# Attention against a small state and a feed-forward block on one core: the order of the first loads and of batch 0's preparation is changed

## The chip, the core and the metric

The kernel runs on one core of a Trainium2 chip. A core has TensorE (PE in the profile: matmuls and transposes), VectorE (DVE), ScalarE (ACT), GpSimd (POOL) and SyncE (SP), each with its own instruction queue that it works off in order, and 16 DMA engines that carry out the transfers which SP, GpSimd and ScalarE issue. The metric is the time of one execution on the device in microseconds: the median of several runs.

## What is computed

For each of B = 8 batches and H = 8 heads, x (512 tokens x 64) attends to a state of 32 rows x 64, and the state attends to x. Both results, 544 rows per batch, go through a feed-forward block with a SiLU.

```python
scores = scale * x @ state.T            # per batch and head
a      = softmax(scores)                # over the 32 state rows
xread  = a @ state                      # 512 rows
a2     = softmax(scale * state @ x.T)   # over the 512 tokens
sread  = a2 @ x                         # 32 rows
y      = concat([xread, sread])         # 544 rows x 512
out    = silu(y @ w_in) @ w_out         # w_in 512 x 2048, w_out 2048 x 512
```

x, state and the weights arrive in fp32, the matmuls run in bf16, and the output is fp32, 4352 x 512.

## The kernel before

The 512 tokens of a batch and the hidden width of 2048 are tiled into 4 token tiles (tt) and 16 hidden tiles (ft) of 128. Instead of computing xread and multiplying it by w_in, the kernel multiplies the state of a batch by w_in first (**W1**, lines 356 to 387: state rows x 2048) and then the attention weights by W1 (**G1**, lines 396 to 430, ending in a SiLU on ScalarE). **G2** (line 432) multiplies by w_out and accumulates over the 16 hidden tiles in PSUM; `store` evicts and writes a token tile. A batch has 32 G1 matmuls and 64 G2 matmuls of 512 columns.

Ahead of that stand, per batch: x in fp32 loaded into the one buffer `x_f` (line 102; `load_x`, line 104, issued by GpSimd), its cast to bf16 (`cast_x`, line 118), its transpose (by TensorE for batches 0 and 1, `pe_transpose_x`, line 203; by a DMA transpose on SP's queue from batch 2 on, `transpose_x`, line 131), the scores (line 252), the exponentials on ScalarE (line 266), the normalization `norm` (line 276: sums and reciprocals on VectorE, the multiplication on GpSimd unless told otherwise) and the transpose of the normalized weights into aT (lines 295 and 300). The 32 state rows of the second result (`sread`, line 309) are gathered over all batches and pass the feed-forward block at the very end.

The schedule is manual: each engine gets its instructions in the order in which the program emits them, and a tile framework adds the waits between engines. So the place of a call in the text sets its place in the queue of its own engine, and no more than that. x_f is one buffer: x of batch b+1 can be loaded only when the casts of batch b have read it. One engine's `pers` buffers hold the states: `st0_f` and `st0_n` for batch 0 alone (loaded by SP ahead of x, line 163), `st_b` for all batches (loaded by GpSimd at line 179, behind the first weights), and `stT`, the transposed states in a block layout, filled by `evict_state` (line 234).

The weights are loaded in pieces by GpSimd, with a conversion to bf16, in this order: w_in 0 to 255, w_out tiles 0 and 1, w_in 256 to 511, w_out 2 and 3, w_in 512 to 1023, w_out 4 to 7, all states, then (behind the first normalization) w_in 1024 to 1535, w_out 8 to 11, w_in 1536 to 2047, w_out 12 to 15, then x of batch 1 (lines 173 to 181 and 492 to 496).

Batch 0 runs in the loop of line 513 with three of its token tiles: at hidden tiles ft 0, 2, 6 and 10 a piece of W1 of batch 0 is made, at 5 all states are transposed by TensorE, at 6 and 8 they are evicted by VectorE, at 9, 11 and 12 three pieces of W1 of batch 1 are made, at 12 VectorE casts x of batch 1 and x of batch 2 is loaded, and at 14 x of batch 1 is transposed. Then follow the scores of batch 1, the fourth token tile (line 553) with the casts and the DMA transpose of x of batch 2 and the load of x of batch 3, and the loop of line 569 over batches 1 to 7, in which the next batch n = b + 1 is prepared at fixed places (tt, ft): scores at (0, 16 - lead), normalization, casts and the next load at (1, 0), the padded copy of x for sread at (1, 4), sread and W1 at (2, 4) and (3, 4), the DMA transpose of x at (3, 8).

`bank` (line 72) deals the PSUM banks a0 to a3 out in turn to scores, W1 pieces and transposes; within the loop of batch 0 it has three, as a0 holds the third token tile. `keep_busy` issues matmuls on zeros.

Of the kernel before, what the change touches and what calls it, by code (L numbers as in the profile page):

```python
# [41 lines left out]
def kernel(  # L42
# [36 lines left out]
    st0_f = pers.tile([NS, H, D], FP32)  # L79
    st0_n = pers.tile([NS, H, D], BF16)  # L80
# [23 lines left out]
    def load_x(b):  # L104
        nc.gpsimd.dma_start(x_f[:], x[b].rearrange("h (p c) d -> p h c d", p=128, c=4))  # L105
# [54 lines left out]
    busy = pers.tile([128, 512], BF16)  # L160
    nc.vector.memset(warm[:], 0.0)
    nc.scalar.activation(warm[:], warm[:], func=EXP, bias=0.0)
    nc.sync.dma_start(st0_f[:], state[0].rearrange("h n d -> n h d"))
    for hg in range(2):
# [4 lines left out]
    nc.vector.memset(busy[:], 0.0)  # L169
    nc.vector.memset(stT[:, 0], 0.0)  # L170
    nc.vector.memset(stT[:, 1:8], 0.0)
    make_identity(nc, ident)
    load_w_in(0, 256)
    load_w_out(0, 2)
    load_w_in(256, 256)
    load_w_out(2, 2)
    load_w_in(512)
    load_w_out(4, 4)
    nc.gpsimd.dma_start(
        st_b[:], state.rearrange("b h (n2 m v) d -> (b h n2) m (v d)", n2=2, m=8)  # L180
    )


    keep_busy(4, psH, "h1")
    copy(nc.vector, st0_n[:], st0_f[:])
    ps0 = bank([128, 4, NS], BF16, "ps_st0")
    for kt in range(4):
        nc.tensor.transpose(
            ps0[:, kt, :], st0_n[:, ds(2 * kt, 2), :], ident[0:NS, 0:NS]
        )  # L190
    for g in range(2):
        for u in range(2):
            copy(
                nc.vector,
                stT[ds(64 * u, 64), 0, ds(2 * g, 2), u ^ g, :],
                ps0[ds(64 * u, 64), ds(2 * g, 2), :],
            )
    keep_busy(5, psH, "h1")
# [18 lines left out]

    cast_x(0, nc.vector, 0, 2, 0, 4)
    cast_x(0, nc.scalar, 2, 2, 0, 4)
    pe_transpose_x(0, 0, 2, lambda sh, dt, nm: psO.tile(sh, dt, tag="o", name=nm))  # L220
    cast_x(0, nc.vector, 0, 2, 4, 4)
    cast_x(0, nc.vector, 2, 2, 4, 4)
# [11 lines left out]
    def evict_state(u, eng):  # L234
        to = stT.rearrange("p b k s (n m v) -> p b k s n m v", n=2, m=8)
        for g in range(2):
            for v in range(2):
                copy(
                    eng,
                    to[ds(64 * u, 64), ds(1, B - 1), ds(2 * g, 2), u ^ g, :, :, v],  # L240
                    st_ps[0][
                        ds(64 * v, 64), :, ds(1, B - 1), ds(2 * g, 2), u, :
                    ].rearrange("p m b k n -> p b k n m"),
                )
# [7 lines left out]
    def scores(b, hg):  # L252
        ps = bank([128, 4, 4, NS], FP32, "ps_sc")
        sc_ps[hg] = ps
        for c in range(4):
            for j in range(2):
                nc.tensor.matmul(  # L257
                    ps[:, c, ds(2 * j, 2), :],
# [7 lines left out]
    def exps(b, hg, n=4):  # L266
        e = epool.tile([128, 4, 4, NS], BF16, tag="exp", name="exp_nat")
        exp_nat[b, hg] = e
        for c in range(0, 4, n):
            nc.scalar.activation(  # L270
                e[:, ds(c, n)], sc_ps[hg][:, ds(c, n)], func=EXP, bias=0.0, scale=SCALE
            )
# [27 lines left out]
    def pe_transpose_a(b, hg, eng):  # L300
# [3 lines left out]
        copy(eng, aT[b][:, hg, :, :], ps[:])  # L304
# [104 lines left out]
    def emit_G1(k):  # L409
# [20 lines left out]
        nc.scalar.activation(g[:, 0:n], ps[:, 0:n], func=SILU, bias=0.0)  # L430
# [51 lines left out]
    pe_transpose_x(0, 1, 2, new_h, (nc.vector, nc.vector), (0,))  # L482
    scores(0, 0)
    exps(0, 0)
    pe_transpose_x(0, 1, 2, new_h, (nc.vector, nc.vector), (1,))
    scores(0, 1)
    exps(0, 1, 2)
    norm(0, 0)
    norm(0, 1, ((nc.vector, 0, 3), (nc.gpsimd, 3, 1)), 2)
# [6 lines left out]
    load_x(1)  # L496
    for i in (1, 2, 0):
        ones_beside_x(i, nc.gpsimd)
    keep_busy(4, psO, "o")
    pe_transpose_a(0, 0, nc.vector)  # L500
    keep_busy(2, psO, "o")
    pe_transpose_a(0, 1, nc.vector)
# [6 lines left out]
    turn[0] = 2  # L509
# [3 lines left out]
    for ft in range(NFT):  # L513
# [4 lines left out]
        if ft == 5:  # L518
            transpose_state()
        if ft == 6:  # L520
            evict_state(0, nc.vector)
        if ft == 8:
            evict_state(1, nc.vector)
        if ft == 12:
            cast_x(1, nc.vector)
            load_x(2)
# [126 lines left out]
```

## Time and profile before

| | us |
|---|---|
| median of 7 runs | 221.33 |
| lowest and highest | 219.98, 224.02 |
| the profiled execution, its own time | 221.62 |
| its span, first to last instruction | 219.8 |

The profile is of one execution. A part of a stage that each engine is busy, and the two chains that lead to the end, are shown with the prediction. Three more facts of the page are of use:

| what | number |
|---|---|
| G2 matmuls (line 438) | 494 recorded, 379 ns each, pipelined |
| HBM read over the span | 17.37 MB |
| DMA transposes of x, issue to landing, least, median and most of six | 3.8, 7.6, 9.8 us |

In such a profile the busy time of an engine says how much it worked, not whether anyone waited for it. In the chain of waits each step is followed back to what released it; in the list of instructions the bracket at the end of a line gives the idle time ahead of the instruction and what ended it. SPq and POOLq are the queues of SP and GpSimd that issue transfers.

### The profile page before, as it was taken

Reading aid. Unit: us, or ns where it says so; the run is one execution under the profiler, and the core shown is the slowest. Engines: PE = TensorE matmul, PEld = TensorE weight load, DVE = VectorE, ACT = ScalarE, POOL = GpSimd, SP = SyncE. Lnnn points to the kernel's source line nnn. Section 1 sums busy time; section 2 is a strip of 40 time slices with the busy share of each in tenths; the row PEclk is TensorE's granted clock in tenths of the full one; section 3 lists DMA queues with packets and bytes.
Section 4 is the critical chain, followed back from the end, with each engine's and each line's share of the span. In section 5 each row is a group of like instructions: output and inputs, shape, how many; then the busy total and the mean of one; then the engine's idle time right before and its main releaser. Section 6 shows DMA issues by size and latency. Waiting matters only on the chain.

```text
span 219.8 us, 3943 instructions
## 1 busy us (share of the span) xinstructions
PE 207.4 (94%) x1577; PEld 97.8 (44%) x1603; DVE 74.4 (34%) x167; ACT 142.6 (65%) x242; POOL 48.3 (22%) x70
## 2 busy tenths in 40 slices
PE   7699899996999999999999999999999999999993
PEld 2334335443444443444444444444444444466662
DVE  5830848301571064306321452136211734200011
ACT  3664579899366975698478938794779666734410
POOL 8490002700820045003700180008000400000000
PEclk9999999999999999999999999999999999999999
DMA  6999955596379025911594158703610331011112
GB/s 185 207 207 206 208 195 162 176 133 205 95 205 223 22 69 125 288 55 48 119 246 121 48 95 237 157 23 113 159 51 0 95 104 48 0 48 51 48 48 95
DMA packets 33489, 27.05 MB, mean 123 GB/s; under 512 B 21440, under 2 KB 27328, under 8 KB 33472
## 3 DMA queue, kind: packets, MB, share of 16 engines
q1 hardware_dynamic: 26656, 15.01, 25.4%
q0 software_dynamic: 6816, 11.80, 24.9%
q8 instruction: 12, 0.20, 0.4%
q14 instruction: 5, 0.04, 0.1%
HBM read 17.37 MB, written 8.91 MB: 120 GB/s over the span
## 4 chain that ended last, share of the span: by engine, by line
PE 78%; DMA 11%; DVE 3%; POOL 2%; issue 2%; ACT 1%; SPq 0%; POOLq 0%
PE o L438 46%; PE h L400 19%; DMA w_in_sb<-in_moe_w_in_dram 5%; DMA xT<-x_nat 4%; PE ps_w L367 4%; PE h L419 3%; DMA x_f<-in_x_dram 2%; PE ps_sc L257 2%; PE o_half L460 2%; DVE stT L149 1%; POOL an L286 1%; PE ps_sr L319 1%; POOL x_nat L149 1%; PE ps_xt L211 1%; DVE W L149 1%
## 5 line engine op out<-in xcount | busy, mean ns | idle before, releaser
L438 PE MATMUL o<-w_out_sb,g 128*128 128x512 bf16 x494 | 132.9, 379 | 2.2 <-issue 1.1
L430 ACT ACTIVATE g<-h 128x512 bf16<-128x512 f32 (+1 forms) x144 | 82.1, 573 | 34.9 <-PE h L400 20.6
L438 PEld LDWEIGHTS <-g 128*128 128x128 bf16 x528 | 49.9, 98 | 59.6 <-issue 6.5
L400 PE MATMUL h<-aT,W 128*128 128x512 bf16 x250 | 74.2, 379 | 0.3
L149 DVE COPY o_sb<-o 128x512 f32<-128x512 f32 x17 | 11.7, 691 | 92.1 <-PE o L438 92.1
L286 POOL TENSOR_TENSOR an<-exp_nat,rc 128x512 bf16<-128x512 bf16 (+2 forms) x16 | 18.5, 1175 | 105.1 <-DVE rc L284 102.2
L400 PEld LDWEIGHTS <-W 128*128 128x128 bf16 x256 | 24.7, 97 | 31.2 <-issue 1.9
L149 DVE CAST W<-ps_w 128x512 bf16<-128x512 f32 (+1 forms) x31 | 20.5, 678 | 35.9 <-PE ps_w L367 35.9
L147 ACT ACTIVATE W<-ps_w 128x512 bf16<-128x512 f32 (+1 forms) x35 | 18.7, 577 | 8.8 <-PE ps_w L367 8.7
L147 ACT ACTIVATE o_sb<-o 128x512 f32<-128x512 f32 x15 | 8.9, 596 | 20.4 <-issue 9.1
L149 POOL CAST x_nat<-x_f 128x512 bf16<-128x512 f32 x24 | 13.7, 606 | 0.9 <-DMA x_f<-in_x_dram 0.9
L367 PE MATMUL ps_w<-w_in_sb,stT 64*32 64x512 bf16 (+1 forms) x264 | 11.4, 376 | 0.8 <-DVE stT L149 0.4
L283 DVE TENSOR_REDUCE rs<-exp_nat 128x16 f32<-128x512 bf16 (+1 forms) x17 | 10.5, 625 | 0.9 <-ACT exp_nat L270 0.2
L105 POOL DMA_DIRECT2D x_f<-in_x_dram x7 | 6.5, 926 | 18.9 <-DVE x_rows L149 17.4
L270 ACT ACTIVATE exp_nat<-ps_sc 128x512 bf16<-128x512 f32 (+1 forms) x17 | 8.8, 569 | 2.0 <-PE ps_sc L257 2.0
L419 PE MATMUL h<-xmT,w_in_sb 128*128 128x256 bf16 x64 | 9.6, 273 | 0.1
L419 PEld LDWEIGHTS <-w_in_sb 128*128 128x128 bf16 x64 | 6.3, 98 | 3.9
L585 ACT ACT_TABLE_LOAD x6 | 7.7, 1283 | 0.1
L270 ACT ACT_TABLE_LOAD x6 | 7.7, 1283 | 0.1
L257 PE MATMUL ps_sc<-stT,xT 128*128 128x64 bf16 x128 | 5.4, 193 | 1.9 <-DMA xT<-x_nat 1.7
L257 PEld LDWEIGHTS <-xT 128*128 128x128 bf16 x128 | 4.8, 98 | 4.2 <-DMA xT<-x_nat 2.2
L155 PE MATMUL ps_busy<-busy 128*128 128x512 bf16 x14 | 5.3, 497 | 1.3 <-DVE busy L169 1.2
(55 smaller groups left out, 86.5 us busy)
## 6 DMA issues: line engine op xcount, KB each, us to landing
out_dram<-o_sb SPq DMA_DIRECT2D x33, 256.0 KB, 2.5
x_f<-in_x_dram POOLq DMA_DIRECT2D x7, 1024.0 KB, 6.9
w_in_sb<-in_moe_w_in_dram POOLq DMA_DIRECT2D x3, 512.0 KB, 10.1
w_out_sb<-in_moe_w_out_dram POOLq DMA_DIRECT2D x3, 512.0 KB, 11.9
x_f<-in_x_dram SPq DMA_DIRECT2D x2, 512.0 KB, 5.0
w_in_sb<-in_moe_w_in_dram POOLq DMA_DIRECT2D x2, 256.0 KB, 6.7
w_out_sb<-in_moe_w_out_dram POOLq DMA_DIRECT2D x2, 256.0 KB, 7.2
st_b<-in_state_dram POOLq DMA_DIRECT2D x1, 256.0 KB, 12.0
```

The lines of the kernel that those rows point to most:

```text
L147: nc.scalar.activation(dst, src, func=COPY, bias=0.0)
L149: eng.tensor_copy(dst, src)
L257: nc.tensor.matmul(ps[:, c, ds(2 * j, 2), :], xT[b][:, c, 2 * hg + j, :], stT[:, b, 2 * hg + j, :, :], start=True, stop=True, skip_group_c ...
L270: nc.scalar.activation(e[:, ds(c, n)], sc_ps[hg][:, ds(c, n)], func=EXP, bias=0.0, scale=SCALE)
L283: nc.vector.tensor_reduce(rs[:, ds(c, nr)], e[:, ds(c, nr)], axis=AX, op=ADD)
L286: eng.tensor_tensor(a[:, ds(c, n)], e[:, ds(c, n)], rc[:, ds(c, n)].to_broadcast([128, n, 4, NS]), op=MULT,)
L367: nc.tensor.matmul(pss[f, hg][ds(32 * s, 32), 0:n], stT[ds(r, 64), b, h // 2, s % 2, :], w_in_sb[ds(r, 64), h // 2, ds(f, n)], start=True, ...
L400: nc.tensor.matmul(h_ps[k][:], W1[b][:, hg, ds(128 * ft, 128)], aT[b][:, hg, :, :], start=(hg == 0), stop=(hg == 1), skip_group_check=True,)
L419: nc.tensor.matmul(ps[:, 0:256], w_in_sb[:, kt, ds(128 * ft, 128)], xmT[:, :, kt].rearrange("p t n b -> p t (n b)"), start=(kt == 0), stop ...
L430: nc.scalar.activation(g[:, 0:n], ps[:, 0:n], func=SILU, bias=0.0)
L438: nc.tensor.matmul(outs[tt][:], gt[b * NFT + ft][:, ds(128 * tt, 128)], w_out_sb[:, ft, :], start=(ft == 0), stop=(ft == NFT - 1), skip_gr ...
L585: nc.scalar.activation(warm[:], warm[:], func=SILU, bias=0.0)
```

## The change

In the head:

- SP's first issue is x of batch 0. State 0 is issued by ScalarE ahead of its table load, in another layout (128 partitions x 2 rows), cast by VectorE, transposed by one matmul and placed into stT by four copies on ScalarE. Seven and two busy matmuls stand where four and five stood.
- The ones beside x of batch 0 are set by GpSimd ahead of the weight loads instead of later.
- State 1 is loaded alone, converted, behind w_out 2 and 3. The load of all states stands behind x of batch 1, which comes as two loads.
- ScalarE casts a quarter more of x of batch 0; both first evictions of its transpose are VectorE's, and of the last two one is ScalarE's. The second half of the scores goes to two PSUM banks, its multiplication wholly to VectorE, and the eviction of its transposed weights is split between VectorE and ScalarE. The SiLU of the first hidden tile is issued in two halves.

In batch 0: state 1 is transposed and placed at ft 4; the pieces of W1 of batch 1 are made at 5, 9 and 11; x of batch 1 is cast in two halves at 13; both its transposes are evicted by VectorE.

In the loop: all states are transposed and evicted in batch 1 at (0, 1); `load_x(3)` stands behind the scores and exponentials of batch 2; the second half of each normalization is multiplied by VectorE; the padded copy stands at (0, 4).

```diff
@@ -76,8 +76,9 @@
 
     ident = pers.tile([128, 128], BF16)
     st_b = pers.tile([128, 8, 2 * D], BF16)
-    st0_f = pers.tile([NS, H, D], FP32)
-    st0_n = pers.tile([NS, H, D], BF16)
+    st0_f = pers.tile([128, 2, D], FP32)
+    st1_n = pers.tile([128, 2, D], BF16)
+    st0_n = pers.tile([128, 2, D], BF16)
 
     stT = pers.tile([128, B, 4, 2, NS], BF16)
     w_in_sb = pers.tile([128, 4, DF], BF16)
@@ -101,8 +102,10 @@
 
     x_f = pers.tile([128, H, 4, D], FP32)
 
-    def load_x(b):
-        nc.gpsimd.dma_start(x_f[:], x[b].rearrange("h (p c) d -> p h c d", p=128, c=4))
+    def load_x(b, h0=0, nh=H):
+        nc.gpsimd.dma_start(
+            x_f[:, ds(h0, nh)], x[b, ds(h0, nh)].rearrange("h (p c) d -> p h c d", p=128, c=4)
+        )
 
     def ones_beside_x(i, eng):
         eng.memset(
@@ -158,44 +161,60 @@
 
     warm = pers.tile([128, 1], FP32)
     busy = pers.tile([128, 512], BF16)
+    nc.vector.memset(busy[:], 0.0)
     nc.vector.memset(warm[:], 0.0)
+    nc.scalar.dma_start(
+        st0_f.rearrange("p v d -> p (v d)"),
+        state[0].rearrange("h (m v) d -> (h m) (v d)", v=2),
+    )
     nc.scalar.activation(warm[:], warm[:], func=EXP, bias=0.0)
-    nc.sync.dma_start(st0_f[:], state[0].rearrange("h n d -> n h d"))
     for hg in range(2):
         nc.sync.dma_start(
             x_f[:, ds(4 * hg, 4), :, :],
             x[0, ds(4 * hg, 4)].rearrange("h (p c) d -> p h c d", p=128, c=4),
         )
-    nc.vector.memset(busy[:], 0.0)
     nc.vector.memset(stT[:, 0], 0.0)
     nc.vector.memset(stT[:, 1:8], 0.0)
     make_identity(nc, ident)
+    ones_beside_x(0, nc.gpsimd)
     load_w_in(0, 256)
     load_w_out(0, 2)
     load_w_in(256, 256)
     load_w_out(2, 2)
+    nc.gpsimd.dma_start(
+        st1_n.rearrange("p v d -> p (v d)"),
+        state[1].rearrange("h (m v) d -> (h m) (v d)", v=2),
+    )
     load_w_in(512)
     load_w_out(4, 4)
-    nc.gpsimd.dma_start(
-        st_b[:], state.rearrange("b h (n2 m v) d -> (b h n2) m (v d)", n2=2, m=8)
-    )
-
-
-    keep_busy(4, psH, "h1")
+
+    def load_states():
+        nc.gpsimd.dma_start(
+            st_b[:], state.rearrange("b h (n2 m v) d -> (b h n2) m (v d)", n2=2, m=8)
+        )
+
+    def transpose_one_state(st):
+        ps = bank([128, 2, 2, 2, 16], BF16, "ps_st1")
+        nc.tensor.transpose(
+            ps.rearrange("p g k u m -> p (g k u m)"), st.rearrange("p v d -> p (v d)"), ident[:]
+        )
+        return ps
+
+    def place_one_state(b, ps, eng):
+        flat = stT.rearrange("p b k s n -> p (b k s n)")
+        to = (
+            flat[0:64, ds(256 * b, 320)].rearrange("p (g w) -> p g w", g=2)[:, :, 0:128],
+            flat[64:128, ds(256 * b + 32, 192)].rearrange("p (g w) -> p g w", g=2),
+        )
+        for u in range(2):
+            by_n = to[u].rearrange("p g (k m v) -> p g k m v", m=16, v=2)
+            for v in range(2):
+                copy(eng, by_n[:, :, 0:3:2, :, v], ps[ds(64 * v, 64), :, :, u, :])
+
+    keep_busy(7, psH, "h1")
     copy(nc.vector, st0_n[:], st0_f[:])
-    ps0 = bank([128, 4, NS], BF16, "ps_st0")
-    for kt in range(4):
-        nc.tensor.transpose(
-            ps0[:, kt, :], st0_n[:, ds(2 * kt, 2), :], ident[0:NS, 0:NS]
-        )
-    for g in range(2):
-        for u in range(2):
-            copy(
-                nc.vector,
-                stT[ds(64 * u, 64), 0, ds(2 * g, 2), u ^ g, :],
-                ps0[ds(64 * u, 64), ds(2 * g, 2), :],
-            )
-    keep_busy(5, psH, "h1")
+    ps0 = transpose_one_state(st0_n)
+    keep_busy(2, psH, "h1")
 
 
 
@@ -215,11 +234,13 @@
                     )
             copy(engs[u], xT[b][:, ds(m * u, m), ds(2 * hg, 2), :], ps[:])
 
+    place_one_state(0, ps0, nc.scalar)
     cast_x(0, nc.vector, 0, 2, 0, 4)
     cast_x(0, nc.scalar, 2, 2, 0, 4)
-    pe_transpose_x(0, 0, 2, lambda sh, dt, nm: psO.tile(sh, dt, tag="o", name=nm))
+    new_o = lambda sh, dt, nm: psO.tile(sh, dt, tag="o", name=nm)
+    cast_x(0, nc.scalar, 2, 2, 4, 4)
+    pe_transpose_x(0, 0, 2, new_o, (nc.vector, nc.vector))
     cast_x(0, nc.vector, 0, 2, 4, 4)
-    cast_x(0, nc.vector, 2, 2, 4, 4)
 
     st_ps = []
 
@@ -237,9 +258,9 @@
             for v in range(2):
                 copy(
                     eng,
-                    to[ds(64 * u, 64), ds(1, B - 1), ds(2 * g, 2), u ^ g, :, :, v],
+                    to[ds(64 * u, 64), ds(2, B - 2), ds(2 * g, 2), u ^ g, :, :, v],
                     st_ps[0][
-                        ds(64 * v, 64), :, ds(1, B - 1), ds(2 * g, 2), u, :
+                        ds(64 * v, 64), :, ds(2, B - 2), ds(2 * g, 2), u, :
                     ].rearrange("p m b k n -> p b k n m"),
                 )
 
@@ -249,13 +270,14 @@
     W1 = {}
     sc_ps = {}
 
-    def scores(b, hg):
-        ps = bank([128, 4, 4, NS], FP32, "ps_sc")
-        sc_ps[hg] = ps
+    def scores(b, hg, m=4):
+        sc_ps[hg] = []
         for c in range(4):
+            if c % m == 0:
+                sc_ps[hg].append(bank([128, m, 4, NS], FP32, "ps_sc"))
             for j in range(2):
                 nc.tensor.matmul(
-                    ps[:, c, ds(2 * j, 2), :],
+                    sc_ps[hg][-1][:, c % m, ds(2 * j, 2), :],
                     xT[b][:, c, 2 * hg + j, :],
                     stT[:, b, 2 * hg + j, :, :],
                     start=True,
@@ -263,13 +285,12 @@
                     skip_group_check=True,
                 )
 
-    def exps(b, hg, n=4):
+    def exps(b, hg):
         e = epool.tile([128, 4, 4, NS], BF16, tag="exp", name="exp_nat")
         exp_nat[b, hg] = e
-        for c in range(0, 4, n):
-            nc.scalar.activation(
-                e[:, ds(c, n)], sc_ps[hg][:, ds(c, n)], func=EXP, bias=0.0, scale=SCALE
-            )
+        n = 4 // len(sc_ps[hg])
+        for i, ps in enumerate(sc_ps[hg]):
+            nc.scalar.activation(e[:, ds(n * i, n)], ps[:], func=EXP, bias=0.0, scale=SCALE)
 
     an = {}
 
@@ -297,11 +318,15 @@
             aT[b][:, hg, :, :], an[b, hg][:].rearrange("p c s n -> p (c s n)")
         )
 
-    def pe_transpose_a(b, hg, eng):
+    def pe_transpose_a(b, hg, eng, other=None):
         ps = bank([128, 4, 128], BF16, "ps_at")
         for c in range(4):
             nc.tensor.transpose(ps[:, c, :], an[b, hg][:, c, :, :], ident[:])
-        copy(eng, aT[b][:, hg, :, :], ps[:])
+        if other is None:
+            copy(eng, aT[b][:, hg, :, :], ps[:])
+        else:
+            copy(eng, aT[b][:, hg, 0:2, :], ps[:, 0:2])
+            copy(other, aT[b][:, hg, 2:4, :], ps[:, 2:4])
 
 
     xm_ps = {}
@@ -427,7 +452,9 @@
         n = 512 if b < B else 256
         g = gpool.tile([128, 512], BF16, tag="g", name="g")
         gt[k] = g
-        nc.scalar.activation(g[:, 0:n], ps[:, 0:n], func=SILU, bias=0.0)
+        m = n // 2 if k == 0 else n
+        for i in range(0, n, m):
+            nc.scalar.activation(g[:, ds(i, m)], ps[:, ds(i, m)], func=SILU, bias=0.0)
 
     def G2(b, tt, ft):
         if ft == 0:
@@ -479,34 +506,37 @@
             done[0] += 1
 
     new_h = lambda sh, dt, nm: psH.tile(sh, dt, tag="h1", name=nm)
-    pe_transpose_x(0, 1, 2, new_h, (nc.vector, nc.vector), (0,))
+    keep_busy(1, psH, "h1")
     scores(0, 0)
     exps(0, 0)
-    pe_transpose_x(0, 1, 2, new_h, (nc.vector, nc.vector), (1,))
-    scores(0, 1)
-    exps(0, 1, 2)
+    keep_busy(1, psH, "h1")
+    pe_transpose_x(0, 1, 2, new_h, (nc.vector, nc.scalar))
     norm(0, 0)
-    norm(0, 1, ((nc.vector, 0, 3), (nc.gpsimd, 3, 1)), 2)
+    scores(0, 1, 2)
+    exps(0, 1)
+    norm(0, 1, ((nc.vector, 0, 4),), 2)
     w1_cols(0, [(0, 256)], (nc.scalar, nc.scalar))
     nc.scalar.activation(warm[:], warm[:], func=SILU, bias=0.0)
     load_w_in(1024)
     load_w_out(8, 4)
     load_w_in(1536)
     load_w_out(12, 4)
-    load_x(1)
-    for i in (1, 2, 0):
+    for hg in range(2):
+        load_x(1, 4 * hg, 4)
+    load_states()
+    for i in (1, 2):
         ones_beside_x(i, nc.gpsimd)
     keep_busy(4, psO, "o")
     pe_transpose_a(0, 0, nc.vector)
-    keep_busy(2, psO, "o")
-    pe_transpose_a(0, 1, nc.vector)
+    keep_busy(1, psO, "o")
+    pe_transpose_a(0, 1, nc.vector, nc.scalar)
     g1_half(0, 0)
     g1_half(1, 0)
 
 
 
     banks[:] = ["a1", "a2", "a3"]
-    turn[0] = 2
+    turn[0] = 0
     W0 = {0: (256, 256), 2: (512, 512), 6: (1024, 512), 10: (1536, 512)}
     LEAD0 = [2, 2, 2, 2, 2, 3, 2, 3, 3, 2, 2, 3, 3, 3, 2, 1]
     ready = 2
@@ -515,21 +545,18 @@
         if ft in W0:
             w1_cols(0, [W0[ft]], both)
             ready = sum(W0[ft]) // 128
-        if ft == 5:
-            transpose_state()
-        if ft == 6:
-            evict_state(0, nc.vector)
-        if ft == 8:
-            evict_state(1, nc.vector)
-        if ft == 12:
-            cast_x(1, nc.vector)
+        if ft == 4:
+            place_one_state(1, transpose_one_state(st1_n), nc.vector)
+        if ft == 13:
+            for hg in range(2):
+                cast_x(1, nc.vector, 0, 4, 4 * hg, 4)
             load_x(2)
-        if ft in (9, 11, 12):
-            w1_chunks(1, ({9: 0, 11: 1, 12: 2}[ft],), both)
+        if ft in (5, 9, 11):
+            w1_chunks(1, ({5: 0, 9: 1, 11: 2}[ft],), both)
         if ft == 14:
             nc.scalar.activation(warm[:], warm[:], func=EXP, bias=0.0)
             pe_transpose_x(1, 0, 1, engs=(nc.vector,))
-            pe_transpose_x(1, 1, 1, engs=(nc.scalar,))
+            pe_transpose_x(1, 1, 1, engs=(nc.vector,))
         if ft < 14:
             for tt in range(3):
                 G2(0, tt, ft)
@@ -558,7 +585,6 @@
             pe_transpose_a(1, 1, nc.vector)
             for c in range(4):
                 cast_x(2, nc.gpsimd, c, 1)
-            load_x(3)
             transpose_x(2)
         if ft >= 14:
             upto(NFT + ft - 12)
@@ -574,6 +600,10 @@
                 at = (tt, ft)
                 if tt == 0:
                     upto(NFT * b + min(lead + ft, NFT))
+                if b == 1 and at == (0, 1):
+                    transpose_state()
+                    for u in range(2):
+                        evict_state(u, nc.vector)
                 if b == B - 1 and at in ((0, 4), (0, 8)):
                     place_xm(at[1] // 8, nc.vector)
                 if n < B:
@@ -583,9 +613,11 @@
                         exps(n, 0)
                         exps(n, 1)
                         nc.scalar.activation(warm[:], warm[:], func=SILU, bias=0.0)
+                        if b == 1:
+                            load_x(3)
                     if at == (1, 0):
                         for hg in range(2):
-                            norm(n, hg)
+                            norm(n, hg, (((nc.gpsimd, nc.vector)[hg], 0, 4),))
                             transpose_a(n, hg)
                         if n + 1 < B:
                             for c in range(4):
@@ -595,7 +627,7 @@
                     if at == (3, 8):
                         if n + 1 < B:
                             transpose_x(n + 1)
-                    if at == (1, 4):
+                    if at == (0, 4):
                         copy(nc.vector, padded(n), x_nat[n][:])
                     if at == (2, 4):
                         if b == 1:
```

## The prediction

> **What bounds the kernel now.** I read four views: the summary and the chain of waits of the page, the busy time by stage, the chain of waits in order of time around 36 to 56 us, and the order of instructions up to 54 us.
>
> ```profile
> span 219.8 us, 3943 instructions
> PE 207.4 (94%) x1577; PEld 97.8 (44%) x1603; DVE 74.4 (34%) x167; ACT 142.6 (65%) x242; POOL 48.3 (22%) x70
> PE 78%; DMA 11%; DVE 3%; POOL 2%; issue 2%; ACT 1%; SPq 0%; POOLq 0%
> ```
>
> TensorE is busy for 94% of the span, and the chain that ended last is 78% TensorE. So time can be won only where TensorE stands still. The stages (length, then busy time of PE, PEld, DVE, ACT, POOL, then clock, DMA share, GB/s) tell where that is not:
>
> ```profile
> 18.00:20.00 2.00, 2.00 (x11) 0.94 (x11) 0.00 (x0) 1.03 (x3) 0.00 (x0) 1.00 1.24 207
> 20.00:22.00 2.00, 1.67 (x21) 0.76 (x19) 0.05 (x1) 0.76 (x3) 0.00 (x0) 1.00 1.24 207
> 50.00:52.00 2.00, 1.06 (x5) 0.29 (x3) 0.00 (x0) 1.88 (x4) 0.00 (x0) 1.00 0.99 323
> 76.00:98.92 22.92, 22.66 (x180) 10.27 (x179) 7.47 (x16) 16.67 (x28) 5.65 (x7) 1.00 0.49 129
> ```
>
> From 53.4 us on a batch takes 22.92 us with TensorE busy for 22.66 of it. The edits to that loop (half of the normalization from GpSimd to VectorE, the padded copy earlier) move work that TensorE does not wait for; I cost them at 0. All that counts lies before 53.4 us. The one long stop there:
>
> ```profile
> 39.73 0.84 issue
> 40.57 0.02 POOLq L105
> 40.58 2.29 POOL x_nat L149 x4
> 42.87 0.02 issue
> 42.89 9.84 DMA xT<-x_nat
> 52.73 0.05 issue
> 52.78 0.64 PE ps_sc L257 x16
> ```
>
> TensorE ends its G1 work at 51.06 and stands for 1.72 us until the transposed x of batch 2 has landed. Followed back: transpose 9.84 us, casts 2.29 us on GpSimd, and these began only at 40.58, when x of batch 2 landed, although GpSimd was free at 39.73. That load could go out only when batch 1 had left the shared buffer x_f:
>
> ```profile
> 32.12 1.23 DVE L149 CAST x_rows<-x_f 128x2048 bf16<-128x2048 f32 x1 [1.34 <-DMA x_f<-in_x_dram]
> 33.65 0.89 POOL L105 DMA_DIRECT2D x_f<-in_x_dram  x1 [17.43 <-DVE x_rows L149]
> ```
>
> VectorE waited for x of batch 1 until 32.12: the start is bound by the bytes that the DMA engines bring (207 GB/s in the stages above, up to some 27 us). So **two chains meet at the scores of batch 2**: the loads (x 1, cast, x 2, cast, transpose) and TensorE's own work. The later one sets the end; all behind it moves by as much.
>
> **Part 1, the load chain.** All states were 256 KB ahead of the later weights and of x of batch 1. Now only state 1 is ahead: 128x128 bf16, 32 KB. 0.262 - 0.033 = 0.229 MB (bf16 size, as the page counts these loads) at 207 GB/s = 1.1 us sooner. The x loads of batch 0 were issued at 1.21 behind 0.41 us of SP's issue of state 0; that goes to ScalarE's queue, so they start 0.47 us sooner. x of batch 1 is there at 32.12 - 1.1 - 0.47 = 30.55. It comes as two loads and is cast as two halves; the first is cast while the second arrives (the W1 eviction queued ahead on VectorE, of tile 11, ends near 29.8). What remains is half of 1.23 us, taken as 0.7 with the fixed part: done at 31.25 instead of 33.35. x of batch 2 goes out 2.1 us sooner and lands at 38.5. Bounds: 0.5 us (the bytes ahead do not set the landing and only the split cast counts) and 2.6 us (the start moves by 1 us).
>
> All states now follow x of batch 1 on GpSimd's queue, landing near 33; TensorE transposes them first in batch 1, near 41: 8 us of cover. State 1 follows 1.05 MB of weights, some 5 us at 207 GB/s after x of batch 0, near 12; it is needed near 18.
>
> **Part 2, the move of x of batch 3 does nothing, I expect.** In the text it stands behind the scores of batch 2. In the instruction list of the changed kernel GpSimd has four casts of batch 2, then this load, then the next multiply: the same order as before, and the load waits for GpSimd and an earlier DMA alone, not for PE or ACT. So it goes out as soon as the casts end (43.16 before, the transpose at 42.89). Here the Trainium skill's "DMA: Bandwidth & Descriptors" (section "Anatomy of one DMA") speaks against the edit: DMA engines do not wait on semaphores; a wait sits in the issuing sequencer before dispatch, so a load without one is not held back. By the edit's intent the transpose would take the median of the six, 7.6 us (they range from 3.8 to 9.8), and land 2.2 us sooner; by row and rule it stays at 9.84. I take 9.84.
>
> **Part 3, the head, up to the first G2 matmul (13.38).** Costs: ScalarE makes four 64x64 copies of state 0 ahead of its cast of x. It has no such row; VectorE's four took 0.80, ScalarE's 128x256 eviction takes 0.39 and its 128x512 0.60, so some 0.2 each, 0.8 in all. Their transpose waits behind seven busy matmuls (four took 1.89, cold, so about 3.0): 4.1 us, copies 4.4 to 5.3, and the cast starts at 5.3 instead of 4.94. Gains: x lands 0.47 sooner, ScalarE shares the casts, VectorE does both first xT evictions, so scores and exps of the first half come about 0.5 sooner; the second xT eviction on ScalarE gives most of that back. The last normalization moves wholly to VectorE (384 columns took 0.70, 256 took 0.61; 512: 0.79) and ends near 10.95, where GpSimd's part ended at 11.31: 0.36 won.
>
> The eviction of the second aT is split over VectorE and ScalarE. Before, one VectorE copy took 0.42. Side by side the halves would take 0.39. The Trainium skill's "PSUM — Partial Sum Buffer" (section "Terms") forbids two engines on the same bank and quadrant at once, and in the instruction list ScalarE's half waits for VectorE's. One after the other: 0.25 + 0.39 = 0.64, so 0.2 lost instead of 0.03 won; I take the loss. The first SiLU in halves (0.39 instead of 0.60) wins 0.2 for the first two G2. Sum 0.36 - 0.2 + 0.2 = 0.4 us; bounds -0.7 (state 0 lands late behind x, and everything on VectorE with it) and 0.9.
>
> **Part 4, batch 0 on TensorE.** Two stops go:
>
> ```profile
> 21.48 0.41 PE L367 MATMUL ps_w<-w_in_sb,stT 64*32 64x512 bf16 x8 [0.33 <-DMA w_in_sb<-in_moe_w_in_dram]
> 25.91 0.41 PE L367 MATMUL ps_w<-w_in_sb,stT 64*32 64x512 bf16 x8 [0.44 <-DVE stT L149]
> ```
>
> The first, because w_in columns 1024 to 1535 land 1.6 us sooner; the second, because W1 of batch 1 needs only state 1 (four copies, 0.8 us, behind one transpose at tile 4) instead of eight copies that ran from 22.56 to 25.85. Seven of eight state transposes leave here: 0.45 us (19.89 to 20.34) less 0.08, so 0.37; all eight return in batch 1 at 0.45. New: W1 of batch 1 at tile 5 and of batch 0 at tile 6 now use the same PSUM bank with only three G2 (0.65 us) between; the second waits for the 0.69 us eviction of the first: 0.3 lost. Sum 0.33 + 0.44 + 0.37 - 0.3 = 0.84; bounds 0.3 and 1.3. The other moves (xT of batch 1 on VectorE alone, cast at tile 13) lie beside G2 work.
>
> **The sum.** TensorE's own chain moves by 0.4 + 0.84 = 1.24: ready for the scores of batch 2 at 51.06 - 1.24 + 0.45 = 50.27. GpSimd has ended the normalization of batch 1 at 39.73 - 1.24 = 38.49; x of batch 2 lands at 38.5. Casts and transpose: 38.5 + 2.3 + 9.85 = 50.65, later than 50.27, so they decide. Scores at 50.7 instead of 52.78: **2.1 us won**, and the steady loop gives nothing back. The profiled execution took 221.62 (span 219.8 and 1.8 around it), the median of seven is 221.33; 221.62 - 2.1 = **219.5 us**. The measurement tells 0.5%, 1.1 us, from no change.
>
> **Rivals.**
> - *The transpose gets free of the load* (0.14). The slowest of six, 9.84, is the one that meets an x load; only a small shift parts them. Then TensorE's chain decides: 52.78 - 50.27 = 2.5, with the better head 2.9: 218.7 to 219.1. Against it: the unchanged order on GpSimd.
> - *x of batch 1 comes no sooner* (0.21): descriptors or GpSimd's issue set its landing, not bytes. Then only the split cast and part of the 0.84 us remain, 0.3 to 1.0 us: 221.0. For it: the last packets of x 1 trickle in at 64 GB/s from 30 to 32 us. Against: a steady 207 GB/s before.
> - *The transpose gets worse* (0.15). Between 46 and 52 us its last packets waited behind x of batch 3: the bulk had moved by 47, the end came at 52.73. VectorE now makes its eight state copies and the padded copy just when GpSimd issues that load. If this drags the load, it drags the transpose's last packets. Each us past 9.84 + 2.1 = 11.9 is lost; at 14 the scores stand at 54.9: 223.7. Against: of six transposes none took over 9.8.
> - The forecast's own case (0.50) spans 218.9 to 220.3.
>
> **Numbers.** Faster by over 0.5%: 0.50 + 0.14 + 0.02 of the second rival = 0.66. Same: 0.19. Slower: 0.15. The range 218.2 to 221.9 holds the forecast and the first two rivals and leaves out the third.
>
> **What would show it.** Right: VectorE's wait for x of batch 1 ends near 30.5; no stop of TensorE at the two W1 pieces; x of batch 2 lands near 38.5; the transpose still takes about 9.8, with a stop of some 0.4 us ahead of the scores. Wrong: x of batch 3 issued only after the exps of batch 2; a first G2 later than 13.4; a batch in the loop other than 22.9 us; a stop at the state transposes of batch 1.

## The result and the profile after

| | us | ratio to before, 95% interval |
|---|---|---|
| before, median in the runs beside the changed kernel (34) | 220.99 | 1 |
| changed kernel, median of 13 runs (218.38 to 222.85) | 218.88 | 0.9915 [0.9896, 0.9934] |
| forecast | 219.5 (218.2 to 221.9) | |
| changed kernel run again, two more sets (e1, e9) | 218.93, 218.96 | 0.9885 [0.985, 0.992], 0.9887 [0.9833, 0.9941] |

The changed kernel is 0.9% faster, 2.1 us by the medians. The first profile taken of it was of a disturbed execution (222.46 us), so the profile shown here is that of the same kernel run again, e1 (its own time 219.18 us). First its page, the span and the engines' busy time:

```profile
span 217.4 us, 3944 instructions
PE 208.2 (96%) x1576; PEld 97.9 (45%) x1602; DVE 77.9 (36%) x174; ACT 143.9 (66%) x248; POOL 42.4 (19%) x65
```

TensorE's share rose from 94% to 96%, on a span that is 2.4 us shorter: the busy time is the same within 1 us, the stops went. The chain of waits in order of time (start, length, what), where the long stop of before was:

```profile
38.30 0.94 issue
...
39.26 2.30 POOL x_nat L152 x4
...
41.58 8.60 DMA xT<-x_nat
...
50.23 0.64 PE ps_sc L279 x16
```

The scores of batch 2 start at 50.23 instead of 52.78. The transpose of x still ends this chain, but TensorE is ready only 0.3 us earlier. By stages (columns as in the prediction), the same two slices of batch 0, the slice with the stop, and one batch of the loop:

```profile
18.00:20.00 2.00, 2.00 (x18) 0.85 (x16) 0.92 (x4) 1.03 (x2) 0.00 (x0) 1.00 1.24 207
20.00:22.00 2.00, 1.81 (x21) 0.53 (x14) 0.98 (x2) 1.39 (x4) 0.00 (x0) 1.00 1.25 206
50.00:52.00 2.00, 1.85 (x23) 1.07 (x23) 0.23 (x1) 1.93 (x3) 0.00 (x0) 1.00 0.18 61
73.26:96.18 22.92, 22.66 (x175) 10.28 (x177) 8.04 (x17) 16.67 (x28) 4.67 (x6) 1.00 0.51 129
```

From 50 to 52 us TensorE is busy for 1.85 us instead of 1.06, and a batch of the loop takes 22.92 us as before. From 20 to 22 us it still misses 0.19 us, where 0.33 were to be won. Where the 2.4 us of the span come from, read off the starts of the first G2 matmul and of the first scores matmul of a batch in the timelines (e9 is the changed kernel with one line moved, which leaves the order in every queue as it is):

| stage | before | e1 | e9 |
|---|---|---|---|
| start to first G2 | 13.38 | 13.05 | 13.14 |
| to the scores of batch 1 | 22.36 | 21.26 | 21.03 |
| to those of batch 2 | 17.04 | 15.92 | 15.60 |
| to those of batch 3 | 23.06 | 23.03 | 23.16 |
| from there to the end | 143.96 | 144.14 | 144.17 |

For e1: 0.33 + 1.10 + 1.12 + 0.03 - 0.18 = 2.4 us.

### The profile page after: what moved, and what is told of

It reads as the page before. It is cut to its first block, busy times and chain, and to the rows that moved or that the text cites. A ratio compares the mean times of both kernels' runs of the same rounds, so it can differ in the third digit from the quotient of the medians.

```text
span 220.7 us, 3944 instructions
## 1 busy us (share of the span) xinstructions
PE 209.8 (95%) x1576; PEld 98.4 (45%) x1602; DVE 78.1 (35%) x174; ACT 143.8 (65%) x248; POOL 42.2 (19%) x65
## 3 DMA queue, kind: packets, MB, share of 16 engines
q1 hardware_dynamic: 26384, 14.95, 24.7%
## 4 chain that ended last, share of the span: by engine, by line
PE 85%; DMA 4%; DVE 3%; issue 3%; POOL 2%; ACT 1%; POOLq 0%; ACTq 0%
PE o L465 48%; PE h L425 22%; DMA xT<-x_nat 4%; PE ps_w L392 4%; PE h L444 3%; PE ps_busy L158 2%; PE ps_sc L279 2%; PE o_half L487 2%; PE ps_sr L344 1%; PE o_a L465 1%; POOL an L307 1%; POOL x_nat L152 1%; DVE W L152 1%; PE ps_xt L230 1%; DVE rs L304 1%
## 5 line engine op out<-in xcount | busy, mean ns | idle before, releaser
L465 PE MATMUL o<-w_out_sb,g 128*128 128x512 bf16 x494 | 134.4, 383 | 1.9 <-issue 1.1
L425 PEld LDWEIGHTS <-W 128*128 128x128 bf16 x256 | 24.7, 97 | 31.5 <-issue 2.0
L307 POOL TENSOR_TENSOR an<-exp_nat,rc 128x512 bf16<-128x512 bf16 (+1 forms) x9 | 9.1, 1013 | 110.4 <-ACT exp_nat L293 73.0
L152 POOL CAST x_nat<-x_f 128x512 bf16<-128x512 f32 x24 | 16.0, 702 | 2.4 <-DMA x_f<-in_x_dram 2.4
L106 POOL DMA_DIRECT2D x_f<-in_x_dram x8 | 7.1, 894 | 17.5 <-DVE x_rows L152 16.0
L158 PE MATMUL ps_busy<-busy 128*128 128x512 bf16 x15 | 6.1, 530 | 1.4 <-DVE warm L165 1.2
```

Source lines behind the costliest of these rows:

```text
L152: eng.tensor_copy(dst, src)
L158: nc.tensor.matmul(ps[:], busy[:, 0:128], busy[:], start=True, stop=True, skip_group_check=True)
L307: eng.tensor_tensor(a[:, ds(c, n)], e[:, ds(c, n)], rc[:, ds(c, n)].to_broadcast([128, n, 4, NS]), op=MULT,)
L425: nc.tensor.matmul(h_ps[k][:], W1[b][:, hg, ds(128 * ft, 128)], aT[b][:, hg, :, :], start=(hg == 0), stop=(hg == 1), skip_group_check=True,)
L465: nc.tensor.matmul(outs[tt][:], gt[b * NFT + ft][:, ds(128 * tt, 128)], w_out_sb[:, ft, :], start=(ft == 0), stop=(ft == NFT - 1), skip_gr ...
```

## The experiments

Theory: the gain comes from the order of the loads and of the states (both chains sooner) and a little from the head; the move of x of batch 3 does nothing. Rivals: the transpose of x of batch 2 was freed from that load; the head alone did it; the loop's edits matter. The kernels were run in three sets (e1 to e4; e5 to e8; e9 to e11), each with runs of the kernel before on the same chip. The last column is read from one profile of each kernel; e4's is of an execution that took 224.31 us.

| kernel | us | ratio, 95% interval | scores of batch 2 at |
|---|---|---|---|
| e1, e9: changed kernel; its load of x of batch 3 put back | 218.93, 218.96 | 0.9885 [0.985, 0.992], 0.9887 [0.9833, 0.9941] | 50.23, 49.77 |
| e2: changed kernel, x of batch 3 really held back | 219.89 | 0.9938 [0.9911, 0.9964] | 49.65 |
| e3: before, x of batch 3 really held back | 220.81 | 0.9971 [0.9945, 0.9997] | 51.37 |
| e4: before with the loop's edits | 220.97 | 0.9979 [0.9952, 1.0006] | 53.44 |
| e5: changed kernel, x of batch 3 issued by SP behind the transpose | 219.38 | 0.9928 [0.9904, 0.9951] | 49.88 |
| e6: before with states, x of batch 1 and W1 as changed | 219.88 | 0.9942 [0.9916, 0.9969] | 50.13 |
| e7: before with the head as changed | 220.6 | 0.9982 [0.9963, 1.0001] | 51.33 |
| e8: changed kernel, second aT evicted whole | no comparison | none | 51.25 |
| e10: e5 and e8 together | 219.22 | 0.9901 [0.9872, 0.9931] | 49.99 |
| e11: e10 with the loop's edits undone | 220.04 | 0.9958 [0.9926, 0.9989] | 49.60 |

**e1: the changed kernel again.**

> The changed kernel once more, for a second profile. Two chains: 218.9 us against 220.9 for the kernel before, ratio 0.991; the transpose of x of batch 2 takes 9 us or more and TensorE stops for 0.4 to 2.4 us ahead of the scores of batch 2. Rival, the gain comes from TensorE's own chain: the stop ahead of those scores has the same length as before (1.7 us) and all the gain is there before the first matmul of batch 1.

It came back within 0.1 us of its first median. The transpose took 8.6 us beside the load of x of batch 3, a little less than expected, and the stop ahead of the scores shrank to 0.3 us without any change of that load's place in GpSimd's queue. The rival asked for a stop as long as before.

**e9: the load put back where it was.**

```diff
             for c in range(4):
                 cast_x(2, nc.gpsimd, c, 1)
+            load_x(3)
             transpose_x(2)
...
-                        if b == 1:
-                            load_x(3)
```

> The changed kernel with the load of x of batch 3 written back at its old place, behind the last GpSimd cast of x of batch 2. Theory: GpSimd's order of instructions is the same either way and the load waits for nothing on TensorE or ScalarE, so the move is empty: the time stays within 0.3% of the changed kernel's (218.4 to 219.4 us, 0.985 to 0.993 of before), the transpose of x of batch 2 takes 8.5 to 9.8 us. Rival (the new place holds the load back): the time rises towards 220 us and the transpose takes longer than in the changed kernel.

218.96 us: no difference. The timeline of e9 (start, length, engine, line, what; in brackets the idle time ahead of it and what ended it):

```profile
30.83 0.69 DVE L152 CAST x_rows<-x_f 128x1024 bf16<-128x1024 f32 x1 [0.24 <-DMA x_f<-in_x_dram]
31.82 0.90 POOL L106 DMA_DIRECT2D x_f<-in_x_dram  x1 [15.61 <-DVE x_rows L152]
38.55 2.28 POOL L152 CAST x_nat<-x_f 128x512 bf16<-128x512 f32 x4 [0.39 <-DMA x_f<-in_x_dram]
40.86 1.79 SPq L137 DMA_TRANSPOSE xT<-x_nat  x1
41.13 0.93 POOL L106 DMA_DIRECT2D x_f<-in_x_dram  x1 [0.30 <-POOL x_nat L152]
```

x of batch 3 (last line) goes out 0.3 us behind the last cast of batch 2, as in e1 (41.85, the casts having begun at 39.26), with the line at the one place or the other. Here x of batch 1 was there 1 us sooner than in e1; the transpose landed by 49.6 and TensorE did not stop. So the load chain differs by about 1 us from one execution to the next with the same order in every queue, and the tie at the scores with it.

**e2 and e3: x of batch 3 held back in earnest.** In both kernels it is issued on ScalarE's queue behind the exponentials of batch 2, so that it does wait:

```diff
                         if b == 1:
-                            load_x(3)
+                            nc.scalar.dma_start(
+                                x_f[:], x[3].rearrange("h (p c) d -> p h c d", p=128, c=4)
+                            )
```

> The changed kernel with x of batch 3 loaded by ScalarE's queue behind the exponentials of batch 2, so that it is really held back. If the last packets of the transpose wait behind that load: the transpose lands in 4 to 7.6 us, no stop of TensorE ahead of the scores of batch 2, 0.5 to 2.3 us less than the changed kernel, 216.6 to 218.4. Rival, the transpose takes over 9 us for another reason (the output store, the transpose itself): no difference, 218.9.

The transpose of batch 2 took 3.7 us, and TensorE did not stop for it: so far the theory is right. Yet the kernel is 1.0 us slower than the changed one, where 0.5 to 2.3 us less were expected. 0.4 us of that stand at the end of the program and have nothing to do with the stop (see e5). The chain of waits of e2 shows the rest, a new stop:

```profile
53.53 1.06 POOL an L307
...
54.61 1.20 SPq L317
...
55.91 5.10 DMA aT<-an
...
61.04 0.38 PE h L425
```

The transpose of the normalized weights, 2.3 us in the median, now meets x of batch 3 and takes 5.10 us; G1 of batch 2 waits 0.86 us. What the edit says it does would have been worse than what it does, by some 0.5 us even without the end.

> The kernel before with this one edit: x of batch 3 on ScalarE's queue behind the exponentials of batch 2. If the load is what keeps the transpose: the stop of 1.72 us ahead of the scores goes, 219.2 us. Rival (the transpose is slow by itself): 220.9, no difference. If TensorE's clock had been falling in that stop in some executions, those above 223 us become rarer as well.

The transpose took 4.5 us instead of 9.8 and the stop went: from the scores of batch 1 to those of batch 2 it took 15.16 us instead of 17.04. The time is a miss all the same, 0.3% instead of the 1.7 us expected. In the profile the gain is eaten up in two places: first G2 is at 14.57, 1.2 us late, as the second half of x of batch 0 was cast 0.5 us later than before and the granted clock was then 0.77 and 0.50 (from 8 to 12 us); and the end of the program takes 0.4 us longer (see e5). The collision seen in e2 costs nothing here: the transposes of the weights took 4.7 and 3.6 us, but TensorE did not wait for them. Whether the other executions lost as much at the head is not known. None of the 12 took over 223 us, of the 29 of the kernel before three did: too few to tell.

**e5: the collision taken away.** x of batch 3 stands on SP's own queue, behind the transpose it disturbed:

```diff
             transpose_x(2)
+            nc.sync.dma_start(x_f[:], x[3].rearrange("h (p c) d -> p h c d", p=128, c=4))
...
-                        if b == 1:
-                            load_x(3)
```

> The changed kernel with x of batch 3 issued by SP right behind the transpose of x of batch 2, on the same queue. If the transpose is only slow because the load of another queue gets between its packets: the transpose lands within 7.6 us, the load after it and ahead of the transposes of the weights of batch 2 (about 54.6), no stop ahead of the scores of batch 2 and none at the first G1 of batch 2: 0.5 to 1.0 us less than the changed kernel, 217.9 to 218.4. Rival, the order on one queue does not part the packets: the transpose still takes 8.5 us or more, 218.9.

Half right. The transpose of x of batch 2 took 3.8 us (view of xT from 38 to 50 us; in e1 the same view says 8.6) and the scores start without a stop (timeline):

```profile
L137 SPq DMA_TRANSPOSE xT<-x_nat x1: 1691/1691/1691, 40.9 to 40.9; - x1
...
DMA to landing us min/median/max: 3.8/3.8/3.8
```

```profile
49.88 0.63 PE L279 MATMUL ps_sc<-stT,xT 128*128 128x64 bf16 x16
```

But the time is not below the changed kernel's. Where TensorE did not stop for x, it started these scores between 49.60 and 49.99 (e2, e5, e9, e10, e11), so some 0.2 to 0.6 us of e1's 50.23 were there to be won. And at the end the kernel loses 0.4 us for another reason. Its last eviction starts 0.1 us sooner than e1's, yet its span is 0.3 us longer (timelines of e1 and of e5):

```profile
213.94 0.42 DVE L152 COPY o_half<-o_half 128x256 f32<-128x256 f32 x1 [1.32 <-PE o_half L487]
```

```profile
213.85 0.42 DVE L152 COPY o_half<-o_half 128x256 f32<-128x256 f32 x1 [1.32 <-PE o_half L487]
```

The trace's rows of SP show that it ends the program by checking nine semaphores one after the other, 0.06 us apart. The last store's is the ninth wherever GpSimd loads x of batch 3, and the second where SP or ScalarE does (e2, e3, e5, e10, e11), presumably because one transfer more on their queues shifts the turn. The other seven are then checked behind its landing: from there to the end of the span it is 1.32 us in e5 and 0.89 in e1. Less these 0.4 us, e5 stands level with the changed kernel.

**e6, e7, e4: the parts alone**, each put on the kernel before. e6: the order of the states, x of batch 1 in two loads, the W1 pieces. e7: the head (state 0, casts, evictions, halves of SiLU). e4: the loop's normalization and padded copy:

```diff
-                            norm(n, hg)
+                            norm(n, hg, (((nc.gpsimd, nc.vector)[hg], 0, 4),))
...
-                    if at == (1, 4):
+                    if at == (0, 4):
                         copy(nc.vector, padded(n), x_nat[n][:])
```

> The kernel before with the states' part alone: state 1 alone, all states behind x of batch 1, x of batch 1 in two loads and two casts, W1 of batch 1 at tiles 5, 9 and 11, states transposed in batch 1. By the sum: x of batch 1 1.1 us sooner and the last cast 0.5 us shorter, TensorE 0.84 us sooner, scores of batch 2 about 51.2: 1.6 us less than before, 0.993. Rival, the gain is in the head: no more than 0.5 us less, 0.998 or above.

> The kernel before with the head's part alone: x of batch 0 first, state 0 by ScalarE, the new division of casts, evictions and normalization, the first SiLU in halves; states, W1 order and loop as before. By the sum: first G2 0.3 to 0.4 us sooner, loads 0.47 us sooner: 0.5 us less than before, 0.998. Rival, the head carries the gain: 1.5 us less or more, 0.993.

> The kernel before with the loop's edits alone: the second half of each normalization on VectorE and the padded copy at (0, 4). The loop is bound by TensorE: no difference, 220.9 within 0.3, a batch stays at 22.9 us. Rival, the loop's edits carry the gain: 219 us.

e6 brings over half: scores of batch 1 at 34.52 and of batch 2 at 50.13 without a stop. e7 brings about 0.4 us, at the edge of what can be told; its chain of waits keeps a stop, of 0.5 us. x of batch 2 lands 0.8 us sooner than before, but still 0.5 later than in e1, and the transpose takes 9.18 us:

```profile
39.80 2.30 POOL x_nat L152 x4
...
42.11 9.18 DMA xT<-x_nat
...
51.33 0.64 PE ps_sc L273 x16
```

e4 cannot be told from no change. The product of the three ratios is 0.9942 * 0.9982 * 0.9979 = 0.9903, beside 0.9915, 0.9885 and 0.9887 for the whole: within their intervals the parts add up, and e4's 0.2% need not be nothing.

**e8 and e10: the split eviction of aT.**

```diff
-    pe_transpose_a(0, 1, nc.vector, nc.scalar)
+    pe_transpose_a(0, 1, nc.vector)
```

> The changed kernel with the second aT evicted by VectorE in one copy. By the bank rule the halves run one after the other (0.42 and 0.38 us in the trace), so one copy of 0.42 us lets the first G2 start 0.3 us sooner, 12.7 instead of 13.04; whether the total follows depends on which chain is later at the scores of batch 2: 218.6 to 218.9. Rival, splitting pays: the first G2 comes later than 13.04.

In the changed kernel ScalarE's half of the second aT waits for VectorE's half, and G1 for ScalarE's (timeline of the changed kernel):

```profile
11.75 0.38 ACT L150 ACTIVATE aT<-ps_at 128x256 bf16<-128x256 bf16 x1 [0.22 <-DVE aT L152]
12.19 0.59 PE L425 MATMUL h<-aT,W 128*128 128x512 bf16 x2 [0.24 <-ACT aT L150]
```

Evicted whole, both aT take VectorE 0.97 us together and first G2 starts at 12.62 (timeline of e8):

```profile
12.62 0.61 PE L465 MATMUL o<-w_out_sb,g 128*128 128x512 bf16 x2
```

That is 0.43 us sooner than in e1. Its runs are too few for a total, and x of batch 2 landed at 40.29, which gave a 1.4 us stop of its own. e10 asks for the total, with e5's cure for that stop:

> The changed kernel with x of batch 3 issued by SP behind the transpose of x of batch 2, and the second aT of the head evicted by VectorE in one copy. Theory (both stops are real, and with the transpose at 7.5 us the loads no longer decide the start of the scores of batch 2): the first G2 matmul at 12.6 instead of 13.05, no TensorE stop for xT, scores of batch 2 at 49.4 to 49.6, and 0.3 to 0.4 us less than with SP's load alone: 218.9 to 219.1 us, 0.991 of before. Rival (the head's gain is swallowed in batch 0 or 1 by a wait for W_in or for a landing): scores of batch 2 at 49.8 or later and 219.3 us, 0.993.

The rival holds. First G2 starts at 12.79, the scores of batch 2 at 49.99 and the time is 219.22. In this profile the gain is lost again in batch 0, at the W1 piece of hidden tile 6 (timelines of e9 and of e10):

```profile
21.08 0.53 PE L392 MATMUL ps_w<-w_in_sb,stT 64*32 64x512 bf16 x8
```

```profile
21.31 0.41 PE L392 MATMUL ps_w<-w_in_sb,stT 64*32 64x512 bf16 x8 [0.51 <-DMA w_in_sb<-in_moe_w_in_dram]
```

e10 comes to this piece sooner and stands 0.51 us for w_in, which lands at 21.27; e9, 0.35 us later at first G2, does not stand at all, as w_in landed at 20.32 there. In e11, whose head and batch 0 are e10's, it landed at 20.43 and there is no stop. So this landing too moves by about 1 us between executions. The three profiles with the whole eviction have first G2 0.3 us sooner on average than e1, e2, e5 and e9, but the scores of batch 1 no more than 0.05 us sooner (34.15 and 34.20). Less the 0.4 us of its end, e10 would stand at 218.8, level with the changed kernel.

**e11: the loop's edits undone in e10.**

> The same, with the loop's normalisation and padded copy as in the kernel before (both halves on GpSimd). In the profiles the 0.3 us that the changed kernel loses between the scores of batches 5 and 6 appear only where half the normalisation is on VectorE; with GpSimd alone the interval was 22.9. Theory (that edit is what costs them): the interval goes back to 22.9 and the time is 0.3 us below that of the run beside it: 218.6 to 218.8 us, 0.990. Rival (the interval has another cause, an output's eviction or store that falls late): it stays at 23.2 to 23.4 and the time is the same within 0.15 us.

Both missed: the time rose by 0.8 us (219.28 to 221.72 beside 218.84 to 219.95; both kernels have the longer end), and the interval between the scores of batches 5 and 6 stayed at 23.16 us. From the scores of batch 2 to those of batch 3 it took 23.77 us, in e10 23.15. The normalization of batch 2 is wholly on GpSimd, and G1 waits for the transpose of the weights (timeline of e11):

```profile
53.49 2.50 POOL L307 TENSOR_TENSOR an<-exp_nat,rc 128x512 bf16<-128x512 bf16 x2 [12.84 <-DVE rc L305]
...
60.58 0.38 PE L425 MATMUL h<-aT,W 128*128 128x512 bf16 x1 [0.46 <-DMA aT<-an]
```

But this transpose was not late: it was issued at 56.02, in e10 at 56.25. It took 4.5 us (view of aT from 55.9 to 57 us), in e10 2.4:

```profile
L317 SPq DMA_TRANSPOSE aT<-an x1: 1191/1191/1191, 56.0 to 56.0; - x1
...
DMA to landing us min/median/max: 4.5/4.5/4.5
```

In e5, with half of the multiplication on VectorE, it took 3.9 us; in e6, with all of it on GpSimd, 2.4. So that e11 is slower is clear from its runs, but why is open: the trace does not show that the place of the normalization made the transpose longer.

In batch 5 there is another wait for aT, 0.17 us in e1 and e9 and 0.66 us in e10, none in before and e6. One guess is the half on VectorE, which lets GpSimd issue the next x sooner (126.71 in e9, 128.06 in e6). e7, whose loop is that of before, speaks against it: there too G1 waits 0.22 us for aT, and the interval is 23.30 us. No version that was run beats the changed kernel, and the changed kernel with the old normalization and nothing else was not run.

## Why the prediction was right, point by point

- **Time, sign and cause: right.** 2.1 us were forecast, 2.1 by the medians came. 219.5 stands 0.6 above the result, as it was made from an execution of 221.62 us and the medians of before are 221.0 to 221.7.
- **Two chains meet at the scores of batch 2: right.** Both had to come forward: in e7, where x of batch 2 lands at 39.8 us, the transpose keeps TensorE waiting until 51.33; in e3, on the kernel before with a transpose of 4.5 us, TensorE's own work keeps them until 51.37.
- **Part 1, sooner loads: the direction right, the size not.** The last cast of x of batch 1 was to end at 31.25. It began at 31.81 in e1, 30.83 in e9 and 31.07 in e5, so it ended between 31.5 and 32.5; before, at 33.35. Some 0.9 to 1.8 us were won instead of 2.1. The sum that was too large is 0.229 MB at 207 GB/s plus the 0.47 us of SP's issue: x of batch 1 came 0.3 to 1.3 us sooner (32.12 before), not 1.57. The parts tell which term: with the states' order alone it landed at 31.05 us in e6 (32.03 before), 1.0 us sooner, close to the 1.1 of the bytes; with the head alone at 31.81 in e7, 0.2 us sooner. x of batch 0 did go out 0.47 us sooner, but its second half landed at 6.70 us in e1 and at 6.71 before. Besides, the landing differs by 1 us between executions of the same program, which one profile could not show.
- **The transpose stays at 9.84: too high.** It took 8.6 in e1 and at most 8.7 in e9. The two errors were of opposite sign, and that the chain ended at 50.23, so near the 50.7 of the forecast, is luck in part.
- **Part 2, the move of x of batch 3 does nothing: right**, by e9. The Trainium skill's "DMA: Bandwidth & Descriptors" (section "Anatomy of one DMA") says that a wait belongs to the sequencer that issues the transfer; e2, where that sequencer is ScalarE behind its exponentials, held the load and e9's GpSimd did not. What the page could not give is the price: really held, it costs 1.0 us, 0.4 of it at the end of the program.
- **Part 3, the head: 0.33 instead of 0.4 us.** The normalization ended at 10.94 in e1, where 10.95 was forecast. Two terms were a little too small: the four copies on ScalarE were to take 0.8 us and took 0.98, and the split eviction was to lose 0.2 us and lost 0.3 on average by first G2 (0.43 between e1 and e8). The rule of "PSUM — Partial Sum Buffer" (section "Terms"), that two engines may not be on one bank and quadrant at once, had the sign right: side by side was not to be had, as ScalarE's half stood 0.22 us for VectorE's.
- **Part 4, batch 0: 1.10 (e1) and 1.33 us (e9) instead of 0.84.** The stop for stT at the piece of batch 1 is gone and the transposes left. The stop for w_in is not simply gone, it sits at hidden tile 6 with 0 to 0.5 us: columns 1024 to 1535 were to land 1.6 us sooner and landed 0.2 (e1) to 1.1 us (e9) sooner, and TensorE comes sooner too. The 0.3 us for the shared PSUM bank did not come: at 21.08 in e9 the second piece starts without a stop.
- **The loop at 0: right for the sum, not in its parts.** From the scores of batch 3 to the end 0.2 us were lost. On the kernel before, the loop's edits cannot be told from nothing (e4); on a faster one they carry 0.8 us (e10 against e11). The forecast said that TensorE does not wait for that work. In e11 it does wait, behind the transpose of the weights; why that transpose is longer there is open.

The rivals: the transpose freed of the load did not come about, since the load was not moved (e9). x of batch 1 did come sooner. The transpose did not get worse.

## What to carry to other kernels

Where two chains end at the same instruction, price both, and expect no more than the smaller of the two gains: here a load chain that came forward by too little kept a stop (e7), and curing it beyond the tie brought nothing that could be told (e5). A transfer is moved only by what its issuing queue waits for, so look at the instruction list of that queue rather than at the text; and before holding a large load back, look at what it will meet later. When a version differs by a few tenths of a microsecond, look at the last lines of both timelines too: here an edit at 42 us lengthened the end of the program by 0.4 us (e5). An edit that brings nothing on the slow version can carry time on a faster one, so try parts on both.

## What the runs showed of the hardware

- The DMA transpose of x of batch 2 took 8.6 to 9.8 us where a 1 MB load of x went out on GpSimd's queue 0.3 us behind it (before, both profiles of the changed kernel, e6 to e9; 10.6 in e4), and 3.7 to 4.5 us where that load stood elsewhere (e2, e3, e5, e10, e11). In e5 the load goes out on SP's queue 1.8 us behind it, 2.0 us before it lands, and it still takes 3.8 us. The transposes of the weights took 3.6 to 5.1 instead of 2.3 us when the load came from ScalarE's queue (e2, e3). The transposes of later batches range from 3.7 to 9.0 us in all kernels, so this load is not all that makes them long.
- In the first profile of the changed kernel TensorE stood for 2.3 us ahead of the scores of batch 2, and the granted clock went from 1.00 to 0.89, 0.50 and 0.76 in the next three slices of 2 us (stages of that profile, columns as above):

```profile
52.00:54.00 2.00, 1.83 (x22) 1.08 (x23) 0.29 (x1) 1.37 (x3) 0.00 (x0) 0.89 0.06 16
54.00:56.00 2.00, 2.00 (x6) 0.63 (x5) 1.93 (x5) 1.20 (x2) 0.56 (x1) 0.50 0.34 130
56.00:58.00 2.00, 2.00 (x8) 0.82 (x7) 0.99 (x2) 0.00 (x0) 2.00 (x3) 0.76 0.16 36
```

  e4 shows the same: a stop of 2.23 us, then 0.53 and 0.62 from 54 to 58 us; the batch behind it took 24.7 us in both. With the stop of 1.72 us in the profile of before, and of 1.43 us in e8, the clock stayed at 1.00 and the batch took 23.06 and 23.16 us, hardly longer than 22.92. But in the head of e3 it fell behind a stop of 1.37 us, in a stretch where TensorE was busy for only 0.63 of 2 us. Whether the length of the stop is the cause was not tried.
